# Prologue loads of a fused attention and FFN kernel: three issuing queues, w_in in one piece, a sketch in eight small tiles

## The chip, the cores and the metric

The kernel runs on one core of a Trainium2 chip. The core has a matrix engine (TensorE, PE in the profile, whose weight loads are listed apart as PEld), a vector engine (VectorE, DVE), a scalar engine (ScalarE, ACT), GpSimd (POOL) and SyncE (SP), which here only issues transfers. Sixteen DMA engines move data between the chip's memory (HBM) and the on-chip memory (SBUF); matmul results go to PSUM, in banks of 512 fp32 columns. The metric is the device time of one execution in microseconds (us); lower is better.

## The reference

For each of 4 batches and 4 heads, with a sequence of 1,088 and a head dimension of 32, the first half is a polynomial-sketch attention without softmax:

```python
def phi(x):                       # S1, S2: (8, 32)
    a = np.einsum('rd,bhsd->bhsr', S1, x)
    b = np.einsum('rd,bhsd->bhsr', S2, x)
    return np.einsum('bhsi,bhsj->bhsij', a, b).reshape(*x.shape[:-1], 64)
q_p, k_p = phi(q), phi(k)
kv = np.einsum('bhsf,bhsd->bhfd', k_p, v)
z = np.sum(k_p, axis=2)
num = np.einsum('bhsf,bhfd->bhsd', q_p, kv)
den = np.einsum('bhsf,bhf->bhs', q_p, z)[..., None] + 1e-06
attn = num / den
```

The four heads of a token are put side by side to a vector x of 128, and the second half is an FFN over all 4,352 tokens, with w_in of 128 x 2048 (1 MB) and w_out of 2048 x 128 (1 MB):

```python
h = np.maximum(x @ w_in, 0.0)
out = (h * h) @ w_out
```

## The kernel before

The FFN dominates. It runs over ten token chunks (list FC), the first of 256 tokens; for each chunk TensorE multiplies 16 slices of w_in with the transposed attention result xT (ffn1, L597), ScalarE and VectorE apply relu (L609, L607) and square (L620, L622), and TensorE accumulates the product with the 16 slices of w_o (ffn2, L641). The attention of later chunks is woven between by a planner (class _Order), which works on estimated durations; its list begins behind the prologue and is the same before and after the change.

The prologue is written out by hand. Each engine runs its instructions in the order of the source, and semaphores between the engines are added by the framework. The steps up to the first FFN matmul, for batch 0 and the first 256 tokens:

1. Loads. S1 on ScalarE's queue; S2, k in two pieces (columns 0 to 512, 512 to 1088), q's first 256 columns, then v on SP's queue. v goes to tile vn in 4 partition groups p, each first for sequence tiles 0 to 4 (64 KB) and then for 4 to 9 (80 KB, p = 3: 48 KB); the very first piece of v is issued by ScalarE. Behind them, in the source after the copy to ss, SP issues q's columns 256 to 640, w_in's quarters 0, 1, 2, w_o's quarters 0 and 1, w_in's quarter 3, w_o's quarters 2 and 3, and q's rest (L707 to L716). Loads of batch 1 follow on SP.
2. TensorE runs matmuls on constants (keep_warm, L692, W0 and W1 of 512 columns) around the small product sp (L703), which ScalarE copies to ss (L706): the sketch matrices for all four heads.
3. VectorE transposes k in four pieces (a_kT0, L290) to kt0 and then q's first 256 columns to qT (a_qT, L296).
4. TensorE makes k's sketch kf in four groups of 2, 2, 3 and 2 sequence tiles (a_kf, L315), four matmuls with 32 stationary columns for each tile; ScalarE copies half of it to kb (L321), and VectorE multiplies the two halves to kp (a_kp0, L331).
5. TensorE makes q's sketch x0 (q0, L756). Its weights sq are block-diagonal, made by two multiplications on POOL (L721): two heads on 64 partitions give 128 output partitions, so four matmuls in all. Head pair y and factor x go to PSUM bank 2x + y. ScalarE copies one factor to qb0 (L767), VectorE multiplies it with the other to qp0 (L774).
6. TensorE accumulates kvp over the nine sequence tiles, from kp and v (a_kv0, L396). VectorE masks it to zb, bd, zm (L789 to L800), TensorE computes the denominator (L816) and numerator (L821), VectorE divides and writes xT's first 256 columns (L837 to L844).
7. POOL casts w_in from fp32 in four quarters (cast_wi, L685; the casts stand in the source behind step 6's first part), one more warming matmul reads the first quarter (L835), and ffn1 starts.

Of the kernel before, what the change touches and what calls it, by code (L numbers as in the profile page):

```python
# [14 lines left out]
def _ap(t: bass.AP, p0: int, np_: int, off: int, free):  # L15
    p = list(t.ap)[0]
    return bass.AP(
        t.tensor, t.offset + p0 * p[0] + off, [[p[0], np_]] + [list(d) for d in free]
    )
# [88 lines left out]
def kernel(  # L108
# [11 lines left out]
    nc = tc.nc  # L120

    B, H, S, D = 4, 4, 1088, 32
    G = S // 32
    NT = (S + 127) // 128
# [3 lines left out]
    GT, G2, LA = 4, 6, 3.5  # L128
    LU = 4
    KC = [(0, 160), (160, 128)]  # L130
    W0, W1, W3 = 5, 3, 1
    ND, QT, WI, KL, QL = 2, 6.0, (1.0, 1.9), (30.0, 8.0), 4.0


# [10 lines left out]
    mult = mybir.AluOpType.mult  # L145
# [10 lines left out]
    psf = ctx.enter_context(tc.tile_pool(name="psf", bufs=2, space=bass.MemoryType.PSUM))  # L156
# [3 lines left out]
    def sb(name, cols, dt=F32, rows=128):  # L160
        return cpool.tile([rows, cols], dt, tag=name, name=name)
# [7 lines left out]
    kT, qT = sb("kT", SP), sb("qT", SP)  # L169
    xT = sb("xT", B * S + SP - S, F32R)  # L170
    w_in32, w_o, w_in = sb("w_in32", 2048), sb("w_o", 2048), sb("w_in", 2048, F32R)
    s_nat, ss, s2f = sb("s_nat", 32, rows=16), sb("ss", 80), sb("s2f", 32)
# [13 lines left out]
    def load_q(eng, b, c0, c1):  # L186
        eng.dma_start(
            qn[b % 2][:, c0:c1],
            bass.AP(q.tensor, q.offset + b * H * S * D + c0, [[G * D, 128], [1, c1 - c0]]),
        )  # L190
# [6 lines left out]
    def load_v(eng, b, p, t0=0, t1=NT):  # L197
        n = 32 * ((t1 if p < 3 else min(t1, NT - 2)) - t0)
        eng.dma_start(
            _ap(vn[b % 2], 32 * p, 32, 32 * t0, [[32 * NT, H], [1, n]]),  # L200
            bass.AP(
                v.tensor, v.offset + b * H * S * D + 32 * first(b, t0, p),
                [[G * D, 32], [S * D, H], [1, n]],
            ),
        )

    def load_wi(eng, c):
        eng.dma_start(
            w_in32[:, 512 * c : 512 * c + 512], moe_w_in[:, 512 * c : 512 * c + 512]
        )  # L210

    def load_wo(eng, c):
        eng.dma_start(
            _ap(w_o, 0, 128, 512 * c, [[128, 4], [1, 128]]),
            bass.AP(
                moe_w_out.tensor, moe_w_out.offset + c * 512 * 128,
                [[128, 128], [128 * 128, 4], [1, 128]],
            ),
        )
# [2 lines left out]
    nc.sync.dma_start(s_nat[8:16, :], S2[:, :])  # L222
    load_k(nc.sync, 0, 0, 512)
    load_k(nc.sync, 0, 512, S)
    load_v(nc.scalar, 0, 0, 0, 4)
    load_q(nc.sync, 0, 0, 256)
    for t0, t1 in ((0, 4), (4, NT)):
        for p in range(0 if t0 else 1, 4):
            load_v(nc.sync, 0, p, t0, t1)

    zero_a = sb("zero_a", 8)
    nc.scalar.copy(zero_a[:, :], nc.const_aps.tensor(0.0, (128, 8), F32))

    sq, sel = sb("sq", 256), sb("sel", 320, rows=16)
    nc.vector.memset(sel[:, :], 0.0)
    nc.gpsimd.memset(_ap(vn[0], 96, 32, 32 * (NT - 2), [[32 * NT, H], [1, 64]]), 0.0)
    nc.gpsimd.memset(vn[0][:, VC : VC + 32], 1.0)
# [2 lines left out]
    kt0 = sb("kt0", SP)  # L240
# [8 lines left out]
    for i in range(2):  # L249
# [5 lines left out]
    own_h, own_q = sb("own_h", 4), sb("own_q", 2)  # L255
# [3 lines left out]
    nc.gpsimd.tensor_copy(  # L259
        _ap(sel, 0, 16, 64, [[80, 4], [1, 16]]), _ap(iden, 0, 16, 0, [[0, 4], [1, 16]])  # L260
    )
    nc.vector.tensor_reduce(
        out=own_h[:, :], in_=_ap(iden, 0, 128, 0, [[32, 4], [1, 32]]), op=add, axis=AX
    )
# [2 lines left out]
        out=own_f[:, :], in_=_ap(iden, 0, 128, 0, [[8, 16], [1, 8]]), op=add, axis=AX  # L267
# [11 lines left out]
    def banks(t_, x, col, n, k=2):  # L279

        return _ap(t_, 0, 128, 512 * x + col, [[512, k], [1, n]])
# [5 lines left out]
    def a_kT0(t0, n):  # L287
        p = 3 if t0 + n > NT - 2 else 4
        i = 32 * (first(0, t0, 1) - first(0, t0, 0))
        nc.vector.transpose(  # L290
            _ap(kt0, 0, 128, 128 * t0, [[32, p], [128, n], [1, 32]]),
            _ap(kn[0], 0, 128, 32 * first(0, t0, 0), [[i, p], [32, n], [1, 32]]),
        )

    def a_qT(b, i0, n):
        nc.vector.transpose(qT[:, 32 * i0 : 32 * i0 + 32 * n], qn[b % 2][:, 32 * i0 : 32 * i0 + 32 * n])  # L296
# [10 lines left out]
                )  # L307


    def a_kf(t0, n, pool, tag):  # L310
        kf = pool.tile([128, 512], F32, tag=tag, name="kf")
        for t in range(n):
            for c in range(4):
                o = 128 * (t0 + t) + 32 * c
                nc.tensor.matmul(  # L315
                    _ap(kf, 32 * c, 32, 32 * t, [[32 * n, 2], [1, 32]]),
                    kt0[:, o : o + 32],
                    sf,
                )
        kb = wpool.tile([128, 32 * 3], F32, tag="kb", bufs=4, name="kb")  # L320
        nc.scalar.copy(kb[:, 0 : 32 * n], kf[:, 32 * n : 64 * n])  # L321
        st["kf", t0] = kf, kb

    def new_kp(b):

        st[b, "kp"] = wpool.tile([128, 64 * NT * H], F32, tag="kp", name="kp")

    def a_kp0(t0, n):

        kf, kb = st["kf", t0]  # L330
        nc.vector.tensor_tensor(  # L331
            out=_ap(st[0, "kp"], 0, 128, 256 * t0, [[64, 4 * n], [8, 8], [1, 8]]),
            in0=_ap(kf, 0, 128, 0, [[8, 4 * n], [1, 8], [0, 8]]),
            in1=_ap(kb, 0, 128, 0, [[8, 4 * n], [0, 8], [1, 8]]),
            op=mult,
        )
# [352 lines left out]
    def keep_warm(n, cols=512):  # L689
        t_ = st["warm"]  # L690
        for _ in range(n):
            nc.tensor.matmul(  # L692
                t_[:, 0:cols],
                nc.const_aps.tensor(1.0, (128, 128), mybir.dt.bfloat16),
                nc.const_aps.tensor(1.0, (128, cols), mybir.dt.bfloat16),
            )
# [7 lines left out]
            sp[32 * h : 32 * h + 32, 0:80], s_nat[:, :], sel[:, 80 * h : 80 * h + 80]  # L704
        )
    nc.scalar.copy(ss[:, :], sp[:, 0:80])  # L706
    load_q(nc.sync, 0, 256, 640)  # L707
    load_wi(nc.sync, 0)
    load_wi(nc.sync, 1)
    load_wi(nc.sync, 2)  # L710
    load_wo(nc.sync, 0)
    load_wo(nc.sync, 1)
    load_wi(nc.sync, 3)
    for c in range(2, 4):
        load_wo(nc.sync, c)
    load_q(nc.sync, 0, 640, S)  # L716
    keep_warm(W1)
    a_kT0(0, 2)
    a_kT0(2, 2)
    for x in range(2):  # L720
        nc.gpsimd.tensor_tensor(  # L721
            out=_ap(sq, 0, 128, 128 * x, [[64, 2], [8, 8], [1, 8]]),
            in0=_ap(ss, 0, 128, 72 - 8 * x, [[0, 2]] + [[[0, 8], [1, 8]], [[1, 8], [0, 8]]][x]),
            in1=_ap(own_q, 0, 128, 0, [[1, 2], [0, 8], [0, 8]]),
            op=mult,
        )
    for h in range(H):
        nc.gpsimd.tensor_copy(
# [4 lines left out]
    for w in sw:  # L733
# [3 lines left out]
        out=_ap(sfk, 0, 128, 0, [[16, 2], [1, 16]]),  # L737
        in0=_ap(ss, 0, 128, 64, [[0, 2], [1, 16]]),
        in1=_ap(own_q, 0, 128, 0, [[1, 2], [0, 16]]),
        op=mult,  # L740
# [4 lines left out]

    a_kT0(4, 3)
    a_kT0(7, 2)
    a_qT(0, 0, 8)


    x0 = att("x0")

    def q0(x):
        for y in range(2):
            r, o = slice(64 * y, 64 * y + 64), 512 * (2 * x + y)
            nc.tensor.matmul(x0[:, o : o + 256], sq[r, 128 * x : 128 * x + 128], qT[r, 0:256])  # L756

    new_kp(0)
    qb0 = wpool.tile([128, 512], F32, tag="qb0", bufs=1, name="qb0")
    qp0 = wpool.tile([128, 512], F32, tag="qp0", bufs=1, name="qp0")  # L760
    a_kf(0, 2, psf, "po")
    a_kf(2, 2, psf, "pg")
    a_kf(4, 3, psf, "po")
    a_kf(7, 2, psf, "pg")
    q0(0)
    q0(1)
    nc.scalar.copy(_ap(qb0, 0, 128, 0, [[256, 2], [1, 256]]), banks(x0, 0, 0, 256))  # L767
    st[0, "kvp"] = psf.tile([128, 512], F32, tag="pg", name="kvp")
    for t0, n in ((0, 2), (2, 2), (4, 3), (7, 2)):
        a_kp0(t0, n)  # L770
        for t in range(t0, t0 + n):
            a_kv0(t)

    nc.vector.tensor_tensor(  # L774
        out=_ap(qp0, 0, 128, 0, [[256, 2], [1, 256]]), in0=banks(x0, 2, 0, 256),
        in1=_ap(qb0, 0, 128, 0, [[256, 2], [1, 256]]), op=mult,
# [10 lines left out]
    for c in range(4):  # L787
        cast_wi(c)
    nc.vector.tensor_tensor(  # L789
        out=_ap(zb, 0, 128, 1, [[65, 2], [32, 2], [1, 1]]),  # L790
        in0=_ap(st[0, "kvp"], 0, 128, 32, [[64, 2], [0, 2], [1, 1]]),
        in1=_ap(own_p, 0, 128, 0, [[0, 2], [1, 2], [1, 1]]),
        op=mult,
    )
    nc.vector.tensor_tensor(
        out=_ap(bd, 0, 128, 0, [[64, 2], [32, 2], [1, 32]]),
        in0=_ap(st[0, "kvp"], 0, 128, 0, [[64, 2], [0, 2], [1, 32]]),
        in1=own, op=mult,
    )
    nc.vector.tensor_tensor(  # L800
        out=_ap(zm, 0, 128, 0, [[16, 2], [8, 2], [1, 8]]),
        in0=_ap(st[0, "kvp"], 0, 128, 32, [[64, 2], [0, 2], [1, 8]]),
        in1=_ap(own_f, 0, 128, 0, [[0, 2], [8, 2], [1, 8]]),
        op=mult,
# [8 lines left out]
    for g in range(2):  # L813
        for y in range(2):
            o = 65 * y + 1 - g
# [18 lines left out]
    for _ in range(W3):  # L834
# [10 lines left out]
        out=xT[:, 0:256], in0=num0[:, 0:256], in1=bc0[:, :], op=mult  # L845
# [5 lines left out]
    tu, t = [], 1.2  # L851
# [215 lines left out]
    for u in range(NU):  # L1067
        ci, c0, n, d0, m = units[u]
        w = n * m
# [92 lines left out]
```

## Time and profile before

| | |
|---|---|
| median of 3 runs | 184.5 us (184.08 to 184.54) |
| the profiled execution's own time | 184.55 us |
| its span | 182.7 us |
| granted TensorE clock | 1.00 |
| first FFN matmul (L597) starts by the chain | 13.11 us |
| DMA: w_in's quarters, issue to landing | 4.3 / 4.8 / 5.4 us (min, median, max) |
| HBM read, written over the span | 8.78 MB, 2.23 MB |

The span is the time from the first to the last instruction of the profiled execution; the device time holds a little more around it. Busy times of engines overlap. The chain of waits goes back from the last instruction to what released each step, and lists how long each piece stood on it. In the timeline a line holds neighbouring instructions of one kind: start, time from the first to the end of the last, engine, source line, operation, output and inputs, and in brackets how long the engine stood idle before them and what ended it. An "x8" of matmuls counts records; an fp32 matmul leaves two.

### The profile page before, as it was taken

How to read it: one execution, taken by the hardware profiler on the slowest of the kernel's cores; microseconds unless marked ns; L12 is line 12 of the kernel's file. 1: busy time of each engine (PE TensorE's matmuls, PEld its weight loads, DVE VectorE, ACT ScalarE, POOL GpSimd, SP SyncE). 2: the span in 40 equal slices, each digit the busy share in tenths (PEclk: the TensorE clock that was granted, in tenths of full speed). 3: DMA queues.
4: the chain of work that ended last, by engine and by line, in shares of the span. 5: the costliest groups of instructions: out<-in, count | busy, mean ns of one | idle time of the engine just before them, and what ended most of it. 6: DMA issues, size and time to landing. Idle time of an engine off the chain costs nothing.

```text
span 182.7 us, 3995 instructions
## 1 busy us (share of the span) xinstructions
PE 178.3 (98%) x1529; PEld 105.3 (58%) x1529; DVE 121.8 (67%) x262; ACT 135.9 (74%) x258; POOL 39.4 (22%) x158
## 2 busy tenths in 40 slices
PE   8999999999999999999999999999999999999992
PEld 2768876755645655555455554545555554555792
DVE  3979969999999961799994335996353334333640
ACT  3329679849948886799937778894777777777990
POOL 5544418438300002570008100500000000000000
PEclk9999999999999999999999999999999999999999
DMA  5999990010029700000030200003003000300111
GB/s 150 225 304 341 298 238 17 4 32 0 0 47 238 179 0 4 4 2 0 0 54 14 43 0 5 0 0 59 0 4 57 0 0 5 52 0 0 32 29 29
DMA packets 24610, 11.26 MB, mean 62 GB/s; under 512 B 17936, under 2 KB 23056, under 8 KB 24592
## 3 DMA queue, kind: packets, MB, share of 16 engines
q1 hardware_dynamic: 24272, 10.89, 24.0%
q8 instruction: 12, 0.20, 0.4%
q10 hardware_dynamic: 320, 0.13, 0.3%
q14 instruction: 6, 0.05, 0.1%
HBM read 8.78 MB, written 2.23 MB: 60 GB/s over the span
## 4 chain that ended last, share of the span: by engine, by line
PE 98%; DVE 0%; issue 0%; ACT 0%; ACTq 0%
PE po L641 61%; PE pg L597 18%; PE nd L550 3%; PE po L636 2%; PE warm L692 2%; PE pol L636 2%; PE qc L303 2%; PE nd L414 1%; PE kvp L396 1%; PE kf L315 1%; PE qc L347 1%; PE kvp L414 1%; PE x L756 1%; PE nd L347 0%; PE den L816 0%; PE x L440 0%
## 5 line engine op out<-in xcount | busy, mean ns | idle before, releaser
L641 PE MATMUL po<-g,w_o 128*128 128x512 f32 (+3 forms) x288 | 122.7, 546 | 0.0
L609 ACT ACTIVATE gt<-pg 128x512 f32<-128x512 f32 (+3 forms) x144 | 75.2, 570 | 31.3 <-PE pg L597 30.8
L641 PEld LDWEIGHTS po<-g,w_o 128*128 128x128 f32 x288 | 53.4, 189 | 31.9 <-issue 24.8
L597 PE MATMUL pg<-xT,w_in 128*128 128x512 f32 (+3 forms) x160 | 70.2, 519 | 0.0
L620 ACT ACTIVATE g<-gt 128x512 f32<-128x512 f32 (+2 forms) x102 | 60.7, 623 | 1.6
L622 DVE TENSOR_TENSOR g<-gt 128x512 f32<-128x512 f32 (+3 forms) x43 | 30.0, 699 | 39.5 <-ACT gt L609 38.8
L597 PEld LDWEIGHTS pg<-xT,w_in 128*128 128x128 f32 x160 | 29.1, 190 | 28.6 <-ACT gt L609 11.5
L510 POOL COPY rd<-rc 32x9 f32<-32x9 f32 (+2 forms) x80 | 19.7, 246 | 26.5 <-DVE rc L502 23.3
L456 POOL COPY kv<-kvt 32x64 f32<-32x64 f32 x48 | 12.7, 264 | 44.7 <-DVE kvt L433 42.5
L519 DVE STREAM_SHUFFLE qa<-qc 128x576 f32<-128x576 f32 (+2 forms) x20 | 11.8, 647 | 0.0
L534 DVE TENSOR_TENSOR qp<-qa,qb 128x576 f32<-128x576 f32 (+2 forms) x20 | 10.8, 605 | 0.0
L482 DVE STREAM_TRANSPOSE qt<-qc 128x576 f32<-128x576 f32 (+2 forms) x10 | 5.8, 611 | 6.2 <-PE qc L347 4.4
L367 DVE TENSOR_TENSOR kp<-fs 128x576 f32<-128x576 f32 x12 | 8.7, 741 | 0.0
L645 DVE STREAM_TRANSPOSE oT<-po 128x512 f32<-128x512 f32 (+3 forms) x9 | 5.9, 653 | 2.1 <-PE po L641 2.1
L550 PE MATMUL nd<-qp,kv 32*32 32x288 f32 (+2 forms) x320 | 6.6, 354 | 0.0
L519 DVE STREAM_SHUFFLE qb<-qc 128x576 f32<-128x576 f32 (+2 forms) x10 | 6.1, 649 | 0.0
L567 DVE TENSOR_TENSOR xT<-nd,bc 128x576 fp32r<-128x576 f32 (+2 forms) x10 | 5.6, 594 | 0.6 <-PE nd L550 0.5
L636 PE MATMUL po<-w_o,g 128*128 128x128 f32 x32 | 5.8, 279 | 0.0
L296 DVE STREAM_TRANSPOSE qT<-qn 128x192 f32<-128x192 f32 (+3 forms) x11 | 5.8, 552 | 0.0
L636 PE MATMUL pol<-w_o,g 128*128 128x128 f32 x32 | 5.7, 275 | 0.0
L560 DVE STREAM_TRANSPOSE bc<-rd 128x576 f32<-128x576 f32 (+2 forms) x10 | 5.7, 596 | 0.0
L550 PEld LDWEIGHTS nd<-qp,kv 32*32 32x32 f32 x320 | 2.9, 103 | 3.6 <-issue 2.4
(106 smaller groups left out, 91.2 us busy)
## 6 DMA issues: line engine op xcount, KB each, us to landing
kn<-in_k_dram SPq DMA_DIRECT2D x3, 544.0 KB, 6.9
qn<-in_q_dram SPq DMA_DIRECT2D x3, 544.0 KB, 7.6
vn<-in_v_dram SPq DMA_DIRECT2D x9, 144.0 KB, 6.3
w_in<-in_moe_w_in_dram SPq DMA_DIRECT2D x4, 256.0 KB, 4.8
w_o<-in_moe_w_out_dram SPq DMA_DIRECT2D x4, 256.0 KB, 5.9
out_dram<-oT SPq DMA_DIRECT2D x12, 64.0 KB, 1.9
out_dram<-oT SPq DMA_DIRECT2D x8, 56.0 KB, 1.8
out_dram<-oT SPq DMA_DIRECT2D x8, 48.0 KB, 1.8
```

Of the source, the lines that this page charges most:

```text
L367: nc.vector.tensor_tensor(out=_ap(st[b, "kp"], 0, 128, 64 * NT * h, [[64, NT], [8, 8], [1, 8]]), in0=_ap(fs, 0, 128, o, [[32, NT], [1, 8], ...
L456: nc.gpsimd.tensor_copy(_ap(st[b, "kv"], 32 * c, 32, 64 * h, [[32, E], [1, 32]]), _ap(st["kvt"], 32 * h, 32, 0, [[64, E], [1, 32]]),)
L510: nc.gpsimd.tensor_copy(st[b, "rd", i0][32 * h : 32 * h + 32, n * c : n * c + n], st["rc"][32 * c : 32 * c + 32, n * h : n * h + n],)
L519: nc.vector.stream_shuffle(in_=banks(st[b, "qc", i0], 2 * x, 0, m), out=_ap(st[b, which, i0], 0, 128, 2 * m * x, [[m, 2], [1, m]]), mask=m ...
L534: nc.vector.tensor_tensor(out=st[b, "qp", i0, e][:, r], in0=st[b, f"qa{e}", i0][:, r], in1=st[b, "qb", i0][:, r], op=mult,)
L550: nc.tensor.matmul(nd[32 * h : 32 * h + 32, 512 * c : 512 * c + m], kv[r, o : o + 32], qp[r, m * h : m * h + m], start=(e == 0), stop=(e = ...
L597: nc.tensor.matmul(st["pg", u][:, n * i : n * i + n], w_in[:, 128 * (d0 + i) : 128 * (d0 + i) + 128], xT[:, c0 : c0 + n],)
L609: nc.scalar.activation(gt[:, 0:w], st["pg", u][:, 0:w], Relu)
L620: nc.scalar.activation(to, of, Square)
L622: nc.vector.tensor_tensor(out=to, in0=of, in1=of, op=mult)
L636: nc.tensor.matmul(po[x // 128][:, 0:128], g[:, x : x + 128], w, start=(d == 0), stop=(d == NB - 1),)
L641: nc.tensor.matmul(po[0][:, 0:n], w, g, start=(d == 0), stop=(d == NB - 1))
```

## The change

The loads of batch 0 are issued by three engines. q's first 640 columns come in one load on SP; v's pieces for tiles 0 to 4 go p = 2, 3 on SP and p = 0, 1 on POOL (behind the two copies to sel), those for tiles 4 to 9 go p = 0, 1 on SP, p = 2 on ScalarE behind the copy to zero_a, p = 3 on ScalarE behind the copy to ss. w_in comes in one load of 128 rows of 8 KB, and w_o's quarters follow it. The four casts stay.

q's sketch x0 uses eight matmuls of 32 partitions (one head) by 64 output partitions. The head h and factor x go to bank 2x + h // 2, partition half (h + 1 - x) mod 2; so the two factors of a head lie in opposite halves, and the copy to qb0 swaps the halves in two instructions. sq has 128 columns, made by two copies.

The last group of kf takes 64 stationary columns for each matmul (4 matmuls for 8). The first kp product stands ahead of qT's transpose in VectorE's order. The keep-warm matmuls between sp and kf are two of 512 columns and one of 384, for three of 512.

```diff
-    W0, W1, W3 = 5, 3, 1
+    W0, W1, W3 = 5, 2, 1
...
     load_k(nc.sync, 0, 0, 512)
     load_k(nc.sync, 0, 512, S)
-    load_v(nc.scalar, 0, 0, 0, 4)
-    load_q(nc.sync, 0, 0, 256)
-    for t0, t1 in ((0, 4), (4, NT)):
-        for p in range(0 if t0 else 1, 4):
-            load_v(nc.sync, 0, p, t0, t1)
+    load_q(nc.sync, 0, 0, 640)
+    for p in range(2, 4):
+        load_v(nc.sync, 0, p, 0, 4)

     zero_a = sb("zero_a", 8)
     nc.scalar.copy(zero_a[:, :], nc.const_aps.tensor(0.0, (128, 8), F32))
-
-    sq, sel = sb("sq", 256), sb("sel", 320, rows=16)
+    load_v(nc.scalar, 0, 2, 4, NT)
+    for p in range(2):
+        load_v(nc.sync, 0, p, 4, NT)
+
+    sq, sel = sb("sq", 128), sb("sel", 320, rows=16)
...
         _ap(sel, 0, 16, 64, [[80, 4], [1, 16]]), _ap(iden, 0, 16, 0, [[0, 4], [1, 16]])
     )
+    for p in range(2):
+        load_v(nc.gpsimd, 0, p, 0, 4)
...
-    def a_kf(t0, n, pool, tag):
+    def a_kf(t0, n, pool, tag, w=32):
         kf = pool.tile([128, 512], F32, tag=tag, name="kf")
         for t in range(n):
-            for c in range(4):
-                o = 128 * (t0 + t) + 32 * c
+            for c in range(0, 128, w):
+                o = 128 * (t0 + t) + c
                 nc.tensor.matmul(
-                    _ap(kf, 32 * c, 32, 32 * t, [[32 * n, 2], [1, 32]]),
-                    kt0[:, o : o + 32],
+                    _ap(kf, c, w, 32 * t, [[32 * n, 2], [1, 32]]),
+                    kt0[:, o : o + w],
                     sf,
                 )
...
     nc.scalar.copy(ss[:, :], sp[:, 0:80])
-    load_q(nc.sync, 0, 256, 640)
-    load_wi(nc.sync, 0)
-    load_wi(nc.sync, 1)
-    load_wi(nc.sync, 2)
-    load_wo(nc.sync, 0)
-    load_wo(nc.sync, 1)
-    load_wi(nc.sync, 3)
-    for c in range(2, 4):
+    load_v(nc.scalar, 0, 3, 4, NT)
+    nc.sync.dma_start(w_in32[:, :], moe_w_in[:, :])
+    for c in range(4):
         load_wo(nc.sync, c)
     load_q(nc.sync, 0, 640, S)
     keep_warm(W1)
+    keep_warm(1, 384)
     a_kT0(0, 2)
     a_kT0(2, 2)
     for x in range(2):
-        nc.gpsimd.tensor_tensor(
-            out=_ap(sq, 0, 128, 128 * x, [[64, 2], [8, 8], [1, 8]]),
-            in0=_ap(ss, 0, 128, 72 - 8 * x, [[0, 2]] + [[[0, 8], [1, 8]], [[1, 8], [0, 8]]][x]),
-            in1=_ap(own_q, 0, 128, 0, [[1, 2], [0, 8], [0, 8]]),
-            op=mult,
+        nc.gpsimd.tensor_copy(
+            _ap(sq, 0, 128, 64 * x, [[8, 8], [1, 8]]),
+            _ap(ss, 0, 128, 72 - 8 * x, [[[0, 8], [1, 8]], [[1, 8], [0, 8]]][x]),
         )
...
     def q0(x):
-        for y in range(2):
-            r, o = slice(64 * y, 64 * y + 64), 512 * (2 * x + y)
-            nc.tensor.matmul(x0[:, o : o + 256], sq[r, 128 * x : 128 * x + 128], qT[r, 0:256])
-
-    new_kp(0)
+        for h in range(H):
+            r, o, p = slice(32 * h, 32 * h + 32), 512 * (2 * x + h // 2), 64 * ((h + 1 - x) % 2)
+            nc.tensor.matmul(
+                x0[p : p + 64, o : o + 256], sq[r, 64 * x : 64 * x + 64], qT[r, 0:256]
+            )
+
...
-    a_qT(0, 0, 8)
...
+    new_kp(0)
     a_kf(0, 2, psf, "po")
+    a_kp0(0, 2)
+    a_qT(0, 0, 8)
     a_kf(2, 2, psf, "pg")
     a_kf(4, 3, psf, "po")
-    a_kf(7, 2, psf, "pg")
+    a_kf(7, 2, psf, "pg", 64)
     q0(0)
     q0(1)
-    nc.scalar.copy(_ap(qb0, 0, 128, 0, [[256, 2], [1, 256]]), banks(x0, 0, 0, 256))
+    for i in range(2):
+        nc.scalar.copy(
+            _ap(qb0, 64 * i, 64, 0, [[256, 2], [1, 256]]),
+            _ap(x0, 64 - 64 * i, 64, 0, [[512, 2], [1, 256]]),
+        )
     st[0, "kvp"] = psf.tile([128, 512], F32, tag="pg", name="kvp")
     for t0, n in ((0, 2), (2, 2), (4, 3), (7, 2)):
-        a_kp0(t0, n)
+        if t0:
+            a_kp0(t0, n)
         for t in range(t0, t0 + n):
             a_kv0(t)
```

More of the change, by code (lines that the diff above doesn't have):

```diff
@@ L205, in load_v @@
         )
[L207 to L210, printed above, removed]
     def load_wo(eng, c):
```

## The prediction

> **What bounds the kernel now.** I read the page's busy times first, then the chain of waits over the first 30 us, then the timeline there, then the stretches with their DMA rates. The profiled execution took 184.55 us, of which the span is 182.7; the runs shown have a median of 184.5 (184.08 to 184.54), so sums against 184.55 stand 0.05 above it. A difference under 0.3% (0.55 us) can't be told from no change here.
>
> From the page, busy times:
>
> ```profile
> PE 178.3 (98%) x1529; PEld 105.3 (58%) x1529; DVE 121.8 (67%) x262; ACT 135.9 (74%) x258; POOL 39.4 (22%) x158
> ```
>
> TensorE is the bound. Nothing in the change touches the FFN's matmuls, so the only thing to win or lose is when the first of them (L597) starts. The chain of waits, start and duration:
>
> ```profile
> 3.48 1.39 PE warm L692 x3
> 4.87 1.01 PE kf L315 x32
> ...
> 5.90 1.06 PE kf L315 x40
> 6.96 1.06 PE x L756 x8
> 8.03 2.25 PE kvp L396 x72
> ...
> 12.18 0.50 PE x L440 x8
> 12.68 0.43 PE warm L835
> 13.11 0.53 PE pg L597 x4
> ```
>
> The reader sees a prologue of 13.11 us, nearly all on TensorE. What feeds it, from the timeline:
>
> ```profile
> 5.17 0.84 DVE L290 STREAM_TRANSPOSE kt<-kn 128x384 f32<-128x384 f32 x2 [0.21 <-DMA kn<-in_k_dram]
> ...
> 5.94 0.40 DVE L296 STREAM_TRANSPOSE qT<-qn 128x256 f32<-128x256 f32 x1
> ...
> 6.26 2.71 DVE L331 TENSOR_TENSOR kp<-kf,kb 128x512 f32<-128x512 f32 x4
> 6.36 1.39 SPq L208 DMA_DIRECT2D w_in<-in_moe_w_in_dram  x3
> ...
> 10.70 0.61 POOL L685 CAST w_in<-w_in 128x512 fp32r<-128x512 f32 x1 [3.52 <-DMA w_in<-in_moe_w_in_dram]
> 11.65 1.26 POOL L685 CAST w_in<-w_in 128x512 fp32r<-128x512 f32 x2 [0.34 <-DMA w_in<-in_moe_w_in_dram]
> 15.00 0.61 POOL L685 CAST w_in<-w_in 128x512 fp32r<-128x512 f32 x1 [2.09 <-DMA w_in<-in_moe_w_in_dram]
> ```
>
> The first quarter of w_in lands at 10.70 and is cast by 11.31, 1.37 us before the warming matmul (L835) reads it. The stretches show the cause of its pace; the last two columns are DMA share and GB/s:
>
> ```profile
> 3.00:5.00 2.00, 2.00 (x20) 0.66 (x23) 0.77 (x2) 0.47 (x3) 1.08 (x4) 1.00 1.03 341
> 6.00:7.50 1.50, 1.50 (x46) 1.36 (x47) 1.50 (x5) 0.60 (x3) 1.07 (x9) 1.00 0.76 171
> 8.50:10.00 1.50, 1.50 (x60) 1.50 (x56) 1.07 (x2) 0.16 (x1) 0.00 (x0) 1.00 0.68 179
> 10.50:12.50 2.00, 1.66 (x32) 1.10 (x28) 1.71 (x8) 0.43 (x2) 1.43 (x3) 1.00 1.08 352
> ```
>
> The DMA engines are full at 341 and 352 GB/s, and a quarter to a third idle in two stretches between.
>
> **The attention path, part by part.** The keep-warm matmuls shrink by a twelfth of 1.39, 0.12 us. The last kf group issues 8 records for 16; at 1.06/40 = 27 ns each that is 0.21. Both end kf earlier, at about 6.7, but buy little: the sketch (L756) next needs qT. VectorE's kt transposes end at 6.01, behind k's second load. Now the first kp product stands ahead of qT: 512 of the 2,304 columns of L331, 2.71 x 2/9 = 0.60. So qT runs from 6.6 to 7.0 and the sketch starts at 7.05, against 6.96. Queued behind that qT are the other three kp products, which ended at 8.97 and still end there (the same instructions in another order) if q has landed by 6.6. Of q 640 columns come at once, 320 KB for 128: 192 KB more at 341 GB/s is 0.6 us past 5.8, when qT could start before at the latest (its row begins at 5.94 without a wait): 6.4, so just in time.
>
> The sketch takes 1.06 us for 8 records on two row groups, four in line on each (0.27 each). Eight 32x64 tiles make 16 records, two in line on each tile: between 0.53 (two in line) and 1.06 (no gain). L440, four row tiles, does 8 records of half the width in 0.50; I take 0.65, near the first end. The sketch ends at 7.70, not 8.03. kvp (2.25) follows; its second kp product is ready at 7.6, its last at 8.97 against its use at about 9.4. So kvp ends at 9.95 and everything up to xT stands 0.33 earlier. ScalarE's qb copy (L767, 0.59) becomes two of 64 partitions: at most 1.18, from 7.7 to 8.9, and VectorE reads them at 8.97: hidden by kp; without that cover 0.59. sq is two 64-wide copies for two 128-wide products (0.40 each): cheaper, hidden.
>
> The first-quarter loads of v for p 0 and 1 go to POOL, which idles 1.53 us before sq. The profile has no load issued from POOL; SP's issues last 0.31 to 1.34. Two are 0.6 to 2.7, so POOL is free at 2.9 to 5.0; sq then ends by 5.5, against 7.05. I take 1 us each, 4.4. Queued behind are irep, sw, sfk and memsets (3.3 us, to 8.2), idle time until the casts. v0's ScalarE load took 3.1 us to land, so these land at 5.0 to 8.1 (taken: 7.5); kvp wants them at 7.7: from nothing to +0.4. ScalarE's two later v loads stand before the ss copy, which waits for TensorE, and in the 1.75 us idle before the first kb: 0.43 each, hidden. They and POOL's share the DMA engines with k's second load; but v0's 64 KB, which were ahead of it, go: 0.2 us either way on all of VectorE's chain, taken as 0.
>
> **The w_in load.** SP issues one load each 0.47 us: w_in was the 11th behind k's at 1.20, and (6.36 - 1.20)/11 = 0.47. Now it is the 7th, issued at 4.5, or at 5.2 if it waits for k's second load (SP's waits show issues that wait for an earlier load). The bytes ahead of it are the same, 1.4 MB of k, q and v. But all four casts now wait for the whole 1 MB. On the pace of before: third quarter landed by 12.3 (the cast at 11.65 x2 runs on at 12.3 without a wait), the fourth straight behind it, 0.65 to 0.95 later as between casts: 12.95 to 13.25. Given back: the stretch 6.0 to 7.5 moved 257 KB that 341 GB/s moves in 0.75, with SP issuing 80 KB each 0.47 us (174 GB/s) there: 0.75 back, since the loads come from three queues. The stretch 8.5 to 10, 179 GB/s, is w_in's first quarter; if its 2 KB rows cause that, up to 0.7 comes back, if not, none; I take 0.35, halfway, since no row separates them. So w_in lands at 13.0 - 0.75 - 0.35 = 11.9; ends 11.3 (or 10.8, if the transfers also lag less between engines) and 13.2.
>
> Cast (0.61) and hand-over (0.05, as from kvp's end to the next read of it), then the warming matmul (0.43): the first FFN matmul at T + 1.09 = 12.99; the attention path alone gives 13.11 - 0.33 = 12.78. The later wins: -0.12. The next casts end at T + 1.3, 1.9 and 2.5 and are read from about T + 2, 3.5 and 5.6 (14.02, 15.6 and 17.7 before): covered. w_o's first quarter, 0.9 behind, is read 1.2 us after the first FFN matmul (14.32 against 13.11), its other quarters come earlier than before. q's rest was issued at 11.13, landed within 7.6 us and is read at 19.3; now it is issued no later.
>
> **Sum: 184.55 - 0.12 = 184.4 us**, no change that can be told. The matmuls from 13 us on shift whole: the order there is fixed, and the next x's chain begins from the same kv.
>
> [...]
>
> **Rivals.**
> *w_in in time* (T at most 11.69): VectorE's path sets the start, 184.55 - 0.33 = 184.2, and with k 0.2 earlier, 184.0; if kf's 0.3 counts too, 183.7. For it: w_in is issued 1.2 to 1.9 us sooner. Against: 1 MB must land before any cast, where 256 KB did.
> *w_in late, the other side*: nothing of 8.5 to 10 returns and half of 0.75, T = 12.6, +0.6, or none, T = 13.2, +1.2: 185.1 to 185.7. One mechanism: the first cast waits for the whole load; it decides from T = 12.02 on (13.11 - 1.09), and slower by 0.3% from 12.6.
> *The sketch gains nothing*, so kvp starts at 8.1: 13.11 + 0.1, 184.6. For it: pairs of row tiles now write the same PSUM bank, which no other matmul of the kernel does; against: their partitions differ. [...]
> *v late from POOL*: issue at 2 us each or more, landing at 9, kvp at 9.05 and +1.0: 185.5. For it: no row of such an issue; against: SP's slowest unblocked issue is 0.72.
>
> **Chances.** Forecast (T 11.7 to 12.4) 0.40, its own range 184.1 to 184.9; w_in in time 0.26, half of it below 183.95; w_in late 0.16; sketch without gain 0.09; v late 0.09. Faster by over 0.3% (below 183.95): 0.13. Slower by over 0.3% (above 185.05): the late w_in 0.16, v late 0.09 and a rest of the forecast's upper side, 0.03: 0.28. Same: 0.59. The range 183.8 to 185.3 leaves out the tips of both sides, some 0.2.
>
> **What would show it.** The casts' first wait for w_in ends at 11.9 with four casts in a row; L835 begins right behind the first. L756: 16 records in about 0.65. kvp begins near 7.7, L331's first group ahead of L296. POOL's two issues under 1.5 us each, nothing waiting for vn. DMA share near 1 from 3 to 12 us. The prediction is wrong if the first L597 starts outside 12.5 to 13.6, or if the time moves by more than that start does.

## The result, and the profile after

The changed kernel takes 191.28 us (median of 6 runs, 188.11 to 192.68), against 184.39 (6 runs, 184.08 to 184.63). The ratio is 1.029, with a 95% interval of 1.026 to 1.033; it is made from the three fastest runs alone, since the other three show a lower granted clock still. The forecast was 184.4, with a range of 183.8 to 185.3: wrong, on the slow side. The profiled execution took 190.73 us, with a span of 188.6.

The chain of waits of the changed kernel (start, duration, what), in its first 25 us:

```profile
4.47 0.43 SPq L706
...
4.95 6.95 DMA w_o<-in_moe_w_out_dram
...
12.04 1.39 PE kvp L394 x40
13.43 0.47 PE den L780 x4
...
17.90 0.85 PE pg L595 x4
...
24.90 0.89 PE nd L548 x51
```

The last of these (nd belongs to the next chunk's attention) stood in the chain of before at:

```profile
19.34 0.89 PE nd L550 x51
```

Before, kvp was one piece from 8.03 to 10.28 and the first FFN matmul stood at 13.11. Now kvp has a second part of 40 records that waits for a transfer, and the FFN starts at 17.90. TensorE's waits name it once more (total, times, longest):

```profile
PE kvp L394 <- DMA w_o<-in_moe_w_out_dram: 2.6, 1, 2.6
```

The name w_o misleads. kvp reads kp and v, not w_o; in the run with w_in in two loads below the same wait is named vn. Which piece of v it was is seen from the timeline (start, first to last end, engine, line, operation):

```profile
2.30 1.26 POOL L199 DMA_DIRECT2D vn<-in_v_dram  x2
...
3.56 0.23 ACT L704 COPY ss<-sp 128x80 f32<-128x80 f32 x1 [0.69 <-PE sp L701]
...
4.47 0.43 SPq L706 DMA_DIRECT2D w_in<-in_moe_w_in_dram  x1
...
5.24 0.32 ACTq L199 DMA_DIRECT2D vn<-in_v_dram  x1
...
7.03 0.45 DVE L294 STREAM_TRANSPOSE qT<-qn 128x256 f32<-128x256 f32 x1 [0.37 <-DMA qn<-in_q_dram]
...
7.62 0.69 PE L747 MATMUL x<-qT,sq 32*64 32x256 f32 x16 [0.40 <-DVE qT L294]
8.32 1.15 PE L394 MATMUL kvp<-vn,kp 128*64 128x64 f32 x32
...
11.66 2.28 POOL L683 CAST w_in<-w_in 128x512 fp32r<-128x512 f32 x4 [4.83 <-DMA w_in<-in_moe_w_in_dram]
...
12.04 1.39 PE L394 MATMUL kvp<-vn,kp 128*64 128x64 f32 x40 [2.57 <-DMA w_o<-in_moe_w_out_dram]
```

ScalarE's second v load (p = 3, tiles 4 to 9) is issued at 5.24, behind w_in's 1 MB (4.47). The transfers' list (KB each, us from issue to landing) has it and its neighbours:

```profile
w_in<-in_moe_w_in_dram SPq DMA_DIRECT2D x1, 1024.0 KB, 7.1
...
vn<-in_v_dram POOLq DMA_DIRECT2D x2, 64.0 KB, 4.8
...
vn<-in_v_dram ACTq DMA_DIRECT2D x1, 48.0 KB, 6.6
```

48 KB took 6.6 us and landed at 11.8, 0.2 behind w_in (11.6). Before, the same piece went out on SP ahead of w_in:

```profile
vn<-in_v_dram SPq DMA_DIRECT2D x1, 48.0 KB, 2.2
```

The second loss stands in the stretches (columns as in the prediction; the third from the end is the granted TensorE clock):

```profile
12.50:14.00 1.50, 1.50 (x38) 1.16 (x35) 0.53 (x5) 0.00 (x0) 1.45 (x3) 0.85 1.14 385
14.00:16.00 2.00, 2.00 (x20) 1.18 (x20) 1.24 (x5) 0.27 (x1) 0.00 (x0) 0.50 1.03 340
...
18.00:20.00 2.00, 2.00 (x39) 1.50 (x39) 1.59 (x5) 1.56 (x3) 0.00 (x0) 0.50 1.00 331
20.00:22.00 2.00, 2.00 (x12) 1.78 (x11) 1.83 (x12) 1.67 (x5) 0.71 (x4) 0.90 1.05 280
```

Behind the wait, the clock is granted at one half for 0.15 x 2 x 1.5 + 6.0 + 0.10 x 2 x 2.0 = 6.85 us (the stretch 16 to 18 reads 0.50 too). The difference of the two profiled executions, 190.73 - 184.55 = 6.18 us, then adds up as follows:

| term | before | after | difference |
|---|---|---|---|
| kvp starts | 8.03 | 8.32 | +0.29 |
| kvp, start to end | 2.25 | 5.11 | +2.86 |
| kvp's end to the first FFN matmul | 2.83 | 4.47 | +1.64 |
| first FFN matmul to the next chunk's nd (L550, L548) | 6.23 | 7.00 | +0.77 |
| nd to the span's end (5.9 of span in all); it arises in the stores behind the last matmul | | | +0.34 |
| around the span | 1.85 | 2.13 | +0.28 |

From nd on the FFN's matmuls stand 5.56 to 5.58 us later than before, up to the last: all of the loss but the last two small terms arises in the first 25 us.

### The profile page after: what moved, and what is told of

It reads as the page before. It is cut to its first block, busy times and chain, and to the rows that moved or that the text cites. A ratio compares the mean times of both kernels' runs of the same rounds, so it can differ in the third digit from the quotient of the medians.

```text
span 188.6 us, 3994 instructions
## 1 busy us (share of the span) xinstructions
PE 180.8 (96%) x1529; PEld 106.9 (57%) x1529; DVE 121.8 (65%) x262; ACT 136.7 (72%) x259; POOL 39.6 (21%) x160
## 4 chain that ended last, share of the span: by engine, by line
PE 92%; DMA 4%; SPq 2%; issue 0%; DVE 0%; ACT 0%; ACTq 0%
PE po L639 59%; PE pg L595 18%; DMA w_o<-in_moe_w_out_dram 4%; PE nd L548 3%; PE po L634 2%; PE pol L634 2%; PE qc L301 2%; PE nd L412 1%; SPq L199 1%; PE qc L345 1%; PE kvp L394 1%; PE kvp L412 1%; PE den L816 1%; PE num L821 0%; PE x L438 0%; SPq L181 0%
## 5 line engine op out<-in xcount | busy, mean ns | idle before, releaser
L595 PE MATMUL pg<-xT,w_in 128*128 128x512 f32 (+3 forms) x160 | 71.0, 525 | 0.0
L595 PEld LDWEIGHTS pg<-xT,w_in 128*128 128x128 f32 x160 | 30.0, 195 | 28.5 <-ACT gt L607 11.5
L508 POOL COPY rd<-rc 32x9 f32<-32x9 f32 (+2 forms) x80 | 19.1, 239 | 34.3 <-DVE rc L500 31.1
L517 DVE STREAM_SHUFFLE qa<-qc 128x576 f32<-128x576 f32 (+2 forms) x20 | 11.8, 647 | 0.0
L548 PE MATMUL nd<-qp,kv 32*32 32x288 f32 (+2 forms) x320 | 6.6, 354 | 0.0
L394 PE MATMUL kvp<-vn,kp 128*64 128x64 f32 x72 | 2.5, 224 | 2.6 <-DMA w_o<-in_moe_w_out_dram 2.6
```

The costliest lines, as they stand in the source:

```text
L508: nc.gpsimd.tensor_copy(st[b, "rd", i0][32 * h : 32 * h + 32, n * c : n * c + n], st["rc"][32 * c : 32 * c + 32, n * h : n * h + n],)
L517: nc.vector.stream_shuffle(in_=banks(st[b, "qc", i0], 2 * x, 0, m), out=_ap(st[b, which, i0], 0, 128, 2 * m * x, [[m, 2], [1, m]]), mask=m ...
L548: nc.tensor.matmul(nd[32 * h : 32 * h + 32, 512 * c : 512 * c + m], kv[r, o : o + 32], qp[r, m * h : m * h + m], start=(e == 0), stop=(e = ...
L595: nc.tensor.matmul(st["pg", u][:, n * i : n * i + n], w_in[:, 128 * (d0 + i) : 128 * (d0 + i) + 128], xT[:, c0 : c0 + n],)
```

## The experiments

**The 48 KB piece on SP.** The changed kernel with that one load moved to the place where it stood before:

```diff
-    for p in range(2):
+    for p in (0, 1, 3):
         load_v(nc.sync, 0, p, 4, NT)
...
-    load_v(nc.scalar, 0, 3, 4, NT)
```

> The changed kernel with the one v piece (p = 3, tiles 4 to 9, 48 KB) issued by SP ahead of w_in instead of by ScalarE; w_in stays one load. Theories A and B both: kvp runs through from about 8.3 and ends near 10.5, the first FFN matmul stands at 13.0 to 13.3, clock 1.00, time 184.2 to 184.8. Rival C (another part is the cause: POOL's loads, the sketch's tiles, or the 1 MB load in itself): the wait in kvp or the time above 187 stays.

Measured: 186.56 us (185.23 to 187.77), ratio to before 1.011 [1.007, 1.015]. In the profiled execution kvp runs in one piece, nothing waits for v, and the clock does not fall. This one load of 48 KB thus carries most of the loss: the ratio falls from 1.029 to 1.011, and between the two profiled executions it is 4.98 of 6.18 us (190.73 - 185.75, of 190.73 - 184.55). The expected 184.2 to 184.8 was missed all the same. A part of what is left shows ahead of kvp, in the timeline of this kernel:

```profile
7.46 0.45 DVE L294 STREAM_TRANSPOSE qT<-qn 128x256 f32<-128x256 f32 x1 [0.80 <-DMA qn<-in_q_dram]
...
8.67 2.32 PE L394 MATMUL kvp<-vn,kp 128*64 128x64 f32 x72
```

q lands at 7.4, and the FFN starts at 13.83. Another part is the clock: three of the eight runs have a mean granted clock of 0.991 and took 187.00 to 187.65 us; of the five at 0.998 to 1.000, four took 185.23 to 186.11 and one 187.77.

**The same piece on ScalarE, but early.** Is it the queue, or that it is issued behind w_in?

```diff
-    load_v(nc.scalar, 0, 2, 4, NT)
+    for p in range(2, 4):
+        load_v(nc.scalar, 0, p, 4, NT)
...
-    load_v(nc.scalar, 0, 3, 4, NT)
```

> The changed kernel with ScalarE's second piece of v (48 KB) issued right behind its first, so ahead of w_in in time; nothing else moved. If what costs is that the piece is queued behind w_in's 1 MB: it lands by 7.5, no kvp matmul waits for it, the clock stays granted at 1.0, and the kernel takes 185 to 187, like the run with the piece on SP. If ScalarE's queue as such is slow, whatever stands ahead of it: it lands at 9 or later and the kernel takes over 188. A third outcome: the issue is held by the semaphore of an earlier load, and ScalarE's copies wait behind it; then the first FFN matmul comes late by what they wait.

Measured: 185.53 us (185.39 to 188.21), ratio 1.006 [1.004, 1.008]; first FFN matmul at 13.62. The list of transfers and the timeline of this kernel:

```profile
vn<-in_v_dram ACTq DMA_DIRECT2D x1, 48.0 KB, 3.5
```

```profile
7.25 0.45 DVE L295 STREAM_TRANSPOSE qT<-qn 128x256 f32<-128x256 f32 x1 [0.66 <-DMA qn<-in_q_dram]
...
8.46 2.32 PE L395 MATMUL kvp<-vn,kp 128*64 128x64 f32 x72
```

Landed in 3.5 us instead of 6.6, no wait in kvp. So it was not ScalarE's queue as such that was slow; being issued behind w_in is what cost.

**w_in in two loads.** The changed kernel, w_in in halves of 512 KB (rows of 4 KB for 8 KB):

```diff
-    nc.sync.dma_start(w_in32[:, :], moe_w_in[:, :])
+    for c in range(2):
+        nc.sync.dma_start(
+            w_in32[:, 1024 * c : 1024 * c + 1024], moe_w_in[:, 1024 * c : 1024 * c + 1024]
+        )
```

> The changed kernel with w_in in two loads (rows of 4 KB), v's 48 KB piece on ScalarE as in the change. Theory A (the piece waits for its turns between w_in's packets, or for the whole load that is already queued on an engine): it lands between, at 9.5 to 11, and the wait in kvp is 0.5 to 1.8 us. Rival B (late because issued behind w_in): it lands near 11.8 as with one load, the wait stays 2.6.

One run, without an interval: 187.56 us. Its chain:

```profile
1.46 3.41 DMA vn<-in_v_dram
...
4.89 6.44 DMA vn<-in_v_dram
...
11.46 1.39 PE kvp L394 x40
```

Its first two lines also show why the piece goes out so late, though the copy to ss ended at 3.8: its issue waited for an earlier load to land, here ScalarE's first piece. (In the changed kernel that piece had landed by 4.6; k's second load landed at 5.2, just ahead of the issue at 5.24, but that the issue waited for it is not shown.) It then took 6.4 us again, landing between w_in's halves (issued at 4.5 and 5.3, landed at 11.1 and 12.4), so it was only the load queued ahead that it came in with. TensorE had run at half the clock from 7.8 to 11.2, which is why the wait itself was only 0.4.

**Small packets.** w_in stays one load, but is written with a gap behind each 512 columns, so that its packets are of 2 KB for 8 KB (the tile w_in32 grows to 2,080 columns, and the casts read it in steps of 520):

```diff
-    nc.sync.dma_start(w_in32[:, :], moe_w_in[:, :])
+    nc.sync.dma_start(
+        _ap(w_in32, 0, 128, 0, [[520, 4], [1, 512]]),
+        bass.AP(moe_w_in.tensor, moe_w_in.offset, [[2048, 128], [512, 4], [1, 512]]),
+    )
```

> The changed kernel with w_in still in one load of 1 MB, but written to a tile whose quarters stand 520 columns apart, so that its packets are of 2 KB where they were of 8 KB. Packet size (if the engines take turns between queues, one packet each): the 48 KB of v from ScalarE, issued at about 5.2, then need a quarter of the time beside w_in; landing at about 8 to 9.5, the kvp matmuls wait 0.5 us or less for them, and the kernel takes 186 to 188. Order (the engines finish the load that was queued first): the piece lands again within 0.3 us of the last of w_in, at 11.5 or later, the wait is 2.3 us or more, and the kernel takes 190 to 193.

Measured: 187.68 us (187.41 and 187.94), ratio 1.018 [1.015, 1.020]. The wait and the transfer:

```profile
PE kvp L394 <- DMA w_o<-in_moe_w_out_dram: 2.4, 1, 2.4
```

```profile
w_in<-in_moe_w_in_dram SPq DMA_DIRECT2D x1, 1024.0 KB, 7.2
...
vn<-in_v_dram ACTq DMA_DIRECT2D x1, 48.0 KB, 6.1
```

Packets a quarter of the size gain the piece 0.5 us, not 3: the theory of turns packet by packet falls. That the piece strictly waits for w_in's end is not right either, but it comes close. The DMA rows of the changed kernel from 9.2 to 10.4 us (packets, MB, share of 16 engines):

```profile
DMA packets 338, 0.42 MB, mean 346 GB/s; under 512 B 133, under 2 KB 303, under 8 KB 303
...
q1 hardware_dynamic: 218, 0.37, 82.4%
q10 hardware_dynamic: 120, 0.04, 13.0%
```

q1 is SP's queue, on which w_o follows w_in: only 35 of its 218 packets here are w_in's, of 8 KB. q10 is ScalarE's: the piece is 128 packets of 384 bytes, and 16 more are of 4 bytes. By the trace's packet records, 114 of w_in's 128 packets had moved by 10.0 us and 42 of the piece's; by 10.4 it was 122 and 115, and the last of both moved at 11.1 and 11.2. So the piece came in as w_in ran out. Whether each engine first finishes its own share of w_in is not settled, as the records don't tell the engines apart. In three profiles the 48 KB, issued 0.8 to 0.9 us behind the 1 MB, landed with it: 0.2 us behind it in the changed kernel and in the next run, 0.4 ahead of it here.

The time of this run was not expected. The wait is nearly that of the changed kernel (2.40 for 2.57), yet it is 3.6 us faster. Its stretches say why:

```profile
12.50:14.00 1.50, 1.50 (x33) 1.22 (x30) 0.83 (x5) 0.27 (x1) 1.50 (x3) 1.00 1.21 303
14.00:16.00 2.00, 1.66 (x24) 1.00 (x21) 1.68 (x5) 0.54 (x2) 0.08 (x1) 1.00 1.05 378
```

The clock stayed at 1.00, and the FFN starts at 15.87, not 17.90. kvp's end to that start is 2.83, and from there to nd 6.22, both as before the change (2.83 and 6.23). So this run is close to the changed kernel's wait without the half clock: 3.3 us (187.68 less 184.35, the kernel before beside it) for the wait and what follows it. In the changed kernel the clock came on top. Its runs with the highest mean granted clocks, 0.996, 0.989 and 0.979, took 188.11, 190.56 and 190.73 us.

**Matmuls in the wait.** Ten matmuls on constants between kvp's fourth and fifth tile, to keep TensorE busy (their PSUM tile den0 is allocated earlier for it):

```diff
         for t in range(t0, t0 + n):
+        if t0 == 4:
+            keep_warm(10)
```

> The changed kernel with ten more matmuls of 512 columns on constants between kvp's first four and last five sequence tiles, so that TensorE is busy while it waits for v; nothing else. If the halved clock (0.50 from 13.6 to 20.4) follows from the idle 2.6 us: the clock stays 1.00, kvp's second part still begins at about 12.0, the first FFN matmul stands at 16.0 to 16.4 instead of 17.9, and the time is 187.3 to 188.0. If the clock is no cause: 190 to 192 as the changed kernel.

Measured: 190.22 us (188.91 to 191.25), ratio 1.028 [1.023, 1.033]: hardly less than the changed kernel, where 187.3 to 188.0 was expected if the clock was a cause. The chain of this kernel:

```profile
8.27 1.16 PE x L747 x16
9.43 1.91 PE kvp L394 x32
11.34 3.23 PE den L690 x10
14.57 1.31 PE kvp L394 x40
...
18.73 0.54 PE pg L595 x4
```

The profiled execution can't answer the question as it was asked. TensorE ran at half pace up to 13.25 us: the sketch took 1.16 for 0.69, kvp's first part 1.91 for 1.15, and the first five of the ten matmuls stood 0.43 apart, the last five 0.22. The clock's rows read 1.00 there, but the trace's first record of the clock is its rise at 13.25. The piece landed at about 13.0, and the ten overran it by 1.6 us. Behind them, at full clock, kvp's end (15.88) to the first FFN matmul is 2.85 and from there to nd 6.23, as before the change (2.83 and 6.23), against 4.47 and 7.00 at half clock. So those 1.64 and 0.77 us are the clock, and the filler was no cure here.

**w_in in quarters, the rest of the change kept.**

```diff
-    nc.sync.dma_start(w_in32[:, :], moe_w_in[:, :])
+    for c in range(4):
+        nc.sync.dma_start(
+            w_in32[:, 512 * c : 512 * c + 512], moe_w_in[:, 512 * c : 512 * c + 512]
+        )
```

> The changed kernel with w_in in four loads of 256 KB (rows of 2 KB) at the same place of SP's queue, ahead of w_o. Theory A (w_in's 8 KB packets hold the DMA engines, and the small packets of v's 48 KB piece on ScalarE's queue get only a turn between them): with 2 KB packets the piece lands by about 9.5, kvp's second part waits under 0.5 us instead of 2.6, clock 1.00, time 184.0 to 185. Rival B (the piece is late because it is issued at 5.24, behind w_in, whatever the packets' size): it still lands near 11.8, time 189 to 192.

Measured: 188.76 us (187.03 to 189.5), ratio 1.021 [1.015, 1.026]. No theory said this: no matmul waits for v, and yet it is slow. Its chain:

```profile
2.08 5.63 DMA qn<-in_q_dram
...
7.73 0.32 ACTq L199
...
8.09 0.22 ACT kb L319
...
9.52 0.69 PE x L750 x16
10.21 3.71 PE kvp L394 x72
```

ScalarE's v issue now waits for q's landing, at 7.7. Queued behind it on ScalarE are the kb copies, and behind those kp, qT and the sketch. Then half clock again (mean 0.51 from 10.7 to 14.2, kvp 3.71 for 2.25):

```profile
10.70:14.20 3.50, 3.50 (x66) 3.27 (x60) 1.65 (x5) 0.77 (x2) 1.74 (x3) 0.51 1.07 319
```

Its runs go by the clock: 187.03 us at a mean granted clock of 1.000, 188.67 and 188.84 at 0.991, 189.50 at 0.982. So a load issued from ScalarE behind its copies cost in two ways here: by landing late, or by holding what is queued behind its issue.

**One load for w_in alone**, in the kernel before:

```diff
-    load_wi(nc.sync, 0)
-    load_wi(nc.sync, 1)
-    load_wi(nc.sync, 2)
-    load_wo(nc.sync, 0)
-    load_wo(nc.sync, 1)
-    load_wi(nc.sync, 3)
-    for c in range(2, 4):
+    nc.sync.dma_start(w_in32[:, :], moe_w_in[:, :])
+    for c in range(4):
         load_wo(nc.sync, c)
```

> The kernel before with only w_in in one load (and w_o's quarters behind it), all v ahead of it on SP's queue. Theory A: no v piece stands beside w_in, so no wait in kvp; the first cast begins at 12 to 12.8 and the first FFN matmul at 13.1 to 13.9, time 184.4 to 185.2. Rival C (the 1 MB load in itself): above 187.

Measured: 187.14 us (185.78 to 187.54), ratio 1.012 [1.008, 1.016]. The chain, and a stretch:

```profile
6.36 6.74 DMA w_in<-in_moe_w_in_dram
...
13.16 0.62 POOL w_in L685
...
13.82 0.50 PE warm L830
14.32 0.47 PE pg L597 x4
```

```profile
15.50:19.00 3.50, 3.32 (x12) 2.77 (x11) 3.33 (x19) 2.60 (x5) 1.16 (x7) 0.51 1.06 307
```

Landing at 13.10, the first FFN matmul 1.22 later: this is the rival *w_in late*, in a kernel without the other parts, with the half clock on top. The median lies where "the 1 MB load in itself" was put (above 187), but by way of the clock: the one run at a mean granted clock of 1.000 took 185.78, 1.2 us over the kernel before (184.59 beside it) for a start 1.21 later, and the three at 0.991 took 186.94 to 187.54. In the change a late w_in was not the cause, as it was issued at 4.47.

**The smaller sketch alone**: the loads of the kernel before, the matmuls and order of the one after (kf, sq, q0 and qb). The edit, seen from the changed kernel:

```diff
-    load_q(nc.sync, 0, 0, 640)
-    for p in range(2, 4):
-        load_v(nc.sync, 0, p, 0, 4)
+    load_v(nc.scalar, 0, 0, 0, 4)
+    load_q(nc.sync, 0, 0, 256)
+    for t0, t1 in ((0, 4), (4, NT)):
+        for p in range(0 if t0 else 1, 4):
+            load_v(nc.sync, 0, p, t0, t1)
...
-    nc.sync.dma_start(w_in32[:, :], moe_w_in[:, :])
+    load_q(nc.sync, 0, 256, 640)
+    load_wi(nc.sync, 0)
...
```

> The kernel before with all its loads as they were (q's 256 columns first, v on SP, w_in in quarters) and only the compute side of the change: eight-tile sketch, 64-wide last kf group, first kp product ahead of qT, 128 columns fewer of keep-warm. If the prediction's attention path holds (sketch 0.65 to 0.70 instead of 1.06, kvp 0.3 earlier): first FFN matmul at 12.7 to 12.9, time 0.2 to 0.5 below the kernel before. If the new sketch costs somewhere (two copies on ScalarE, the order on VectorE): no gain or slower.

Measured: 184.66 us (184.35 to 185.02), ratio 1.001 [0.999, 1.003]. In the profiled execution the sketch took 0.69 us, but k's second piece landed at 5.6 for 5.1, and the sketch began at 7.54. No gain that can be told, and no loss.

**What makes q late.** Three runs that begin from the piece on SP. First, POOL's two loads on SP as well, behind p = 2 and 3:

```diff
-    for p in range(2, 4):
+    for p in (2, 3, 0, 1):
         load_v(nc.sync, 0, p, 0, 4)
...
-    for p in range(2):
-        load_v(nc.gpsimd, 0, p, 0, 4)
```

> The run with the 48 KB piece of v on SP, with POOL's two v loads also on SP, behind p = 2 and 3; q still 640 columns in one load, w_in whole. There q landed at 7.4, 0.8 us behind VectorE's wish. Theory P (the v pieces on POOL's and ScalarE's queues pass q on the DMA engines): q lands by 6.7, the sketch starts by 7.2. Theory S (320 KB for 128 is the cause): q still lands at 7.2 or later. w_in is issued 0.9 later, so it lands near 13 and the first FFN matmul stands at 14 to 14.5 either way; time 186.5 to 187.5.

Second, with POOL's loads, q's first 256 columns as a load of their own:

```diff
-    load_q(nc.sync, 0, 0, 640)
+    load_q(nc.sync, 0, 0, 256)
...
+    load_q(nc.sync, 0, 256, 640)
     nc.sync.dma_start(w_in32[:, :], moe_w_in[:, :])
```

> The run with the 48 KB piece of v on SP, with q's first 256 columns in a load of their own and columns 256 to 640 just ahead of w_in; POOL's loads stay. Theory S: q's first load lands by 6.3 and the sketch starts at about 7.0. Theory P: it still lands after 6.8. w_in whole, landing near 12.6, so the first FFN matmul stands near 13.8 and the time stays at 185.5 to 187 under both.

Third, both:

```diff
-    load_q(nc.sync, 0, 0, 640)
-    for p in range(2, 4):
+    load_q(nc.sync, 0, 0, 256)
+    for p in (2, 3, 0, 1):
         load_v(nc.sync, 0, p, 0, 4)
...
-    for p in range(2):
-        load_v(nc.gpsimd, 0, p, 0, 4)
...
+    load_q(nc.sync, 0, 256, 640)
     nc.sync.dma_start(w_in32[:, :], moe_w_in[:, :])
```

> The changed kernel's matmuls and its w_in in one load, with nothing of v on POOL, v's last piece on SP, and q's first 256 columns as a load of their own ahead of v. Expected from the two runs that did one of these each (first FFN matmul at 13.16 and at 12.89 against 13.11): q lands by 5.9, the sketch starts at 7.1, kvp ends by 10.1, w_in lands by 12.0 and the first FFN matmul starts at 12.8 to 13.1: 184.2 to 184.8, no difference that can be told. If the TensorE stall that the run with 256 columns showed at 22 to 23.5 us belongs to the earlier start, it is there again, and the kernel takes 185.0 to 185.6. If the eleventh issue on SP makes w_in late (landing after 12.6), the first FFN matmul starts after 13.6 and the kernel takes over 185.

| kernel | v loads on POOL | q's first load | qT starts | w_in issued, landed | first FFN matmul | time, ratio |
|---|---|---|---|---|---|---|
| piece early on ScalarE | 2 | 320 KB | 7.25 | 5.18, 12.0 | 13.62 | 185.53, 1.006 [1.004, 1.008] |
| piece on SP | 2 | 320 KB | 7.46 | 5.17, 12.6 | 13.83 | 186.56, 1.011 [1.007, 1.015] |
| first | 0 | 320 KB | 6.79 | 6.78, 11.7 | 13.16 | 185.01, 1.003 [1.000, 1.006] |
| second | 2 | 128 KB | 6.54 | 5.59, 11.2 | 12.89 | 185.36, 1.005 [1.002, 1.008] |
| third | 0 | 128 KB | 6.47 | 6.43, 11.7 | 12.98 | 185.08, 1.005 [1.003, 1.006] |

The line of qT in the first's timeline, and in the third's:

```profile
6.79 0.45 DVE L292 STREAM_TRANSPOSE qT<-qn 128x256 f32<-128x256 f32 x1 [0.21 <-DMA qn<-in_q_dram]
```

```profile
6.47 0.42 DVE L292 STREAM_TRANSPOSE qT<-qn 128x256 f32<-128x256 f32 x1
```

The size of q's first load matters: with 128 KB qT does not wait for it, with or without POOL's loads (6.54 and 6.47). That POOL's loads delay q is not shown. 7.46 and 6.79 differ by 0.7, but five of the profiles here have the same loads ahead of w_in, POOL's among them (the changed kernel, small packets, halves, filler, quarters), and in them the 320 KB land anywhere from 6.6 to 7.7; in the first, w_in also goes out 1.6 us later. With the small first load the sketch starts at 7.1 to 7.3 and the FFN 0.13 to 0.22 earlier than before: the gain that the forecast had claimed is there, but it is too small to show. That w_in would land near 13 in the first and near 12.6 in the second did not come true (11.7 and 11.2). The second lost its 0.22 again in a stall of TensorE at 22.7 to 23.5 us that the other profiles of the table don't have; the third's profiled execution was the fastest of its nine (184.71), so the profile doesn't show what the other eight lose. Both stay open. No kernel here beat the one before.

## Why the prediction was wrong

*The step that failed* is the sentence on ScalarE's two later v loads, "0.43 each, hidden". It priced the issue and never asked when the data land and who waits. For POOL's two loads both were asked (landing 5.0 to 8.1, kvp wants them at 7.7); for the 48 KB of p = 3 they were not, though kvp reads them from its fifth tile on, at 9.5. Three things were at hand: in the trace of before an issue of SP's waited 2.0 us for an earlier load, and the same was to be asked of ScalarE's; the load stood in the source right ahead of w_in, but on another queue, so nothing kept it ahead in time (it went out at 5.24, w_in at 4.47); and 1 MB at the 341 GB/s of the stretch is an estimated 3.1 us of transfer. The measured price is 2.57 us of waiting. The first L597 (L595 now) was to stand at 12.5 to 13.6 and stood at 17.90.

*What follows a wait* was missing altogether. The forecast moved the start of the FFN and shifted all else whole. A wait of 2.57 us cost 2.57 and then 1.64 + 0.77 for the clock, so the time moved by 6.18 where the start moved by 4.79: the sign "if the time moves by more than that start does" came true. The half clock lasted 0.49 x 2 x 3.5 = 3.43 us in the run with quarters and in the one with w_in whole, and about twice that, 6.85, in the changed kernel. The fall did not come within the wait: in the changed kernel TensorE had been busy again from 12.04, 1.5 us before the clock fell (at 14.0 - 0.45 = 13.55, by the stretch's 0.85); the last section has the busy times ahead of each fall.

*The sketch*: 0.65 forecast, 0.69 measured, in every profile where it ran at full clock. The rival in which the sketch gains nothing (1.06) fell; 0.69 against the 0.53 of two in line leaves at most 0.16 us for any cost of two row tiles in one bank here.

*q*: 6.4 forecast, 7.0 measured. It was counted by its own bytes at the full rate; with the same loads ahead it landed from 6.6 to 7.7, and what moves it within that stays open. So the sketch began at 7.62, not 7.05, and its gain was gone before v mattered.

*POOL's issues*: 1 us each taken, 1.26 for both; landing 4.8 us after issue, and no matmul waited for them. The rival *v late from POOL* fell, but what it feared came true for the piece from ScalarE.

*w_in*: landing at 11.9 forecast, 11.6 measured (its first cast began at 11.66). That it came so near is in part luck: with the same loads it landed at 12.8 in the filler's run. The reason given for 0.75 of it, that "the loads come from three queues", is not borne out: with nothing on POOL w_in is issued 2.3 us later (6.78) and lands at 11.7 all the same, in 5.0 us for 7.1. As far as one profile of each goes, issuing sooner from more engines did not make the bytes come sooner. Why w_in whole in the kernel before needs 6.7 us, and 5.3 us behind almost the same loads in the third of the q runs, stays open.

*T + 1.09*: 1.22 measured in the kernel before with w_in whole, where it decided. In the changed kernel it never did: by it the FFN could have started at 12.8.

*The bound* was read rightly in the main: 4.79 of the 6.18 us stand before the first FFN matmul and 0.77 before nd, and what the prologue loses is not made up in the remaining 160 us.

## What to carry to other kernels

For every load that a change moves, write down when it is issued, when it lands and who reads it first, also where its issue is hidden; a small load that another queue issued just behind a large one arrived with the large one here (48 KB issued 0.77 us behind 1 MB landed 0.2 us behind it). The source order across two queues was no order in time here, as the piece that stood ahead of w_in went out at 5.24 and w_in at 4.47: what kept the small one ahead in these runs was a place ahead on the same queue, or an early issue that nothing held. A wait of TensorE in the prologue cost more than its length here: behind 2.57 us of waiting the clock was at half for 6.85 us, and the loss was 6.18.

## What the runs showed of the hardware

The half clock lasted 3.4 us in three kernels (3.43 by the stretches with quarters and with w_in whole, 3.40 with halves) and 6.85 us in the changed one, and shorter waits than that went ahead of it. TensorE's longest wait was 1.5 us in the kernel before with w_in whole:

```profile
PE warm L830 <- POOL w_in L685: 1.5, 1, 1.5
```

and its clock fell, while a wait of 2.40 us in the kernel with small packets did not make it fall. TensorE's busy time (by the stretches' PE column) in the 3.41 us ahead of each fall, taken as long as the shorter half clocks:

| kernel | clock falls at (us) | TensorE busy, of the 3.41 us ahead |
|---|---|---|
| quarters | 10.78 | 1.26 |
| changed kernel | 13.56 | 1.52 |
| halves | 7.81 | 1.85 |
| before, w_in whole | 15.55 | 1.92 |

The kernel with small packets was less busy for as long without a fall: of the 3.41 us from 8.24 to 11.65 its wait alone takes 2.40, which leaves at most 1.01, and the clock stayed at 1.00. So neither the length of a wait nor the busy time of such a stretch tells by itself whether the clock falls in these runs; what decides it is not shown, and some matmul records can be missing. In the changed kernel TensorE was busy for 3.07 of the first 3.41 us at half clock and for all of the rest. Why the changed kernel's runs go from 188.11 to 190.73 us stays open too: only the last of these has a trace.

The 1.00 that rows and tables give for the first microseconds is no measurement. In the kernel before the trace's first record of the clock is its rise at 6.58, and the warming matmuls of 512 columns ahead of it stand 0.43 us apart, as ahead of the rise in the filler's run, against 0.22 behind it.

Beside the clock: an issue of a load was held until another load had landed (7.71 for ScalarE's in the run with quarters), and the copies behind it on that engine waited too (4.3 us there). Two v loads issued by POOL took 0.55 and 0.71 us on that engine.
